# Head 0 of an attention kernel transposed on TensorE and written zero-padded, TensorE run with dummy matmuls during the first loads, and VectorE's tiles of head 0 chosen by rotation

## The chip, the cores and the metric

The kernel runs on one core of a Trainium2 chip. The metric is the device time of one execution, in microseconds (us); every figure called a time is the median of several executions. A *span* is the length of one profiled execution, about 1.7 us shorter than the time measured for the same execution. All runs of this study were in the fast state, so fast runs are compared with fast runs throughout.

Five engines matter: TensorE (PE in the profile; PEld are its weight loads), VectorE (DVE), ScalarE (ACT), GpSimd (POOL) and SyncE (SP), which here only issues DMA transfers.

## The reference

32 heads, 2048 queries and 2048 keys of 20 numbers each. Queries and keys are normalised, the scores are scaled by one number t per head, and an ordinary softmax and the product with the values follow.

```python
qn = q / (jnp.sqrt((q * q).sum(axis=-1, keepdims=True)) + eps)
kn = k / (jnp.sqrt((k * k).sum(axis=-1, keepdims=True)) + eps)
logits = jnp.einsum('bhqd,bhkd->bhqk', qn, kn) * t[None, :, None, None]
attn = _softmax(logits, axis=-1)
return jnp.einsum('bhqk,bhkd->bhqd', attn, v)
```

Because of the normalisation no score exceeds t in size, so the kernel takes exponentials without subtracting a maximum. 32 x 2048 x 2048 exponentials are the bulk of the work.

## The kernel before

Scores are made transposed: 128 keys on the partitions, 512 queries along the free axis. A head has 16 key blocks (index r) and 4 query groups (index g), so 64 pieces of 128 x 512. ScalarE takes the exponential of three pieces at a time (a *wave*, 1536 columns, out of PSUM). For 3 or 4 of the 16 key blocks VectorE does it instead, by integer arithmetic on fp16 bit patterns: one pass from PSUM (`xt`), four more in SBUF (`ee`, `ss`, `mm`, `tt`). I call the four pieces of one key block a *VectorE tile*. In the profiles `psA` holds scores for ScalarE, `psD` scores for VectorE, `p_ring` ScalarE's exponentials and `psO` the products with the values.

```python
DVE_TILES = [4 if h % 8 in (1, 4, 6) else 3 for h in range(H)]
...
    if h == 0:
        A_units += [(0, 4 * c + (g + dl) % 4, g) for dl in range(4) for c in range(na // 4) for g in range(NG)]
        rest = range(na // 4 * 4, na)
    else:
        rest = range(na)
    A_units += [(h, r, g) for r in rest for g in range(NG)]
    D_tiles += [(h, r) for r in range(na, R)]
```

A row of a transposed head has only 20 numbers, padded to 32, so four blocks are stacked on the 128 partitions. Key block r = 4c + rho lies in band rho, query group g in band g. A pair with rho = g can be multiplied directly. All other pairs need the keys *rotated* into another band (`kR`). A score matmul may use 32, 64 or 128 rows of the array; with more than 32 the queries come from `qz`, which holds group g in band g and zeros elsewhere.

```python
def qk_mm(eng, h, r, g, dst, rows):
    c, rho = divmod(r, 4)
    dl = (rho - g) % 4
    ...
    mov = qz[bt][ps, g, :] if rows > 32 else qkT[bt][ps, 0:512]
    if dl == 0:
        lhsT = qkT[bt][ps, 512 + 128 * c:512 + 128 * c + 128]
    else:
        lhsT = kR[bt][ps, dl - 1, 128 * c:128 * c + 128]
    return eng.matmul(dst, lhsT, mov, tile_position=(p0, 0))
```

Head 0 has nothing to hide behind. Before, its keys, queries and rotated keys are transposed by three DMA transposes, its first five waves are 32-row matmuls (`WPLAIN = 5`), and GpSimd clears the padding of all buffers:

```python
z_kx = memset("POOL", kx[...][:, :, D:32], 0.0, 0.8, -99)
z_qkn = [memset("POOL", qkn[i][:, :, D:32], 0.0, 0.4, -98 + i) for i in range(NN)]
z_qz = [memset("POOL", qz[i][:, :, :], 0.0, 1.8, -80 + i) for i in range(NT)]
...
trn[0] = add("SP", "trnq0", lambda e, tk: e.dma_start_transpose(
    qkT[0][:, 0:512].rearrange(...), qkn[0][:, 0:R, :].rearrange(...)), 1.3, [nq], -21, lat=2.2, dma="T0")
rot[0].append(add("SP", "trnr0", lambda e, tk: e.dma_start_transpose(
    kR[0][...], kx[:, 512:2048]), 1.3, cp, -20, lat=2.7, dma="R0"))
```

The order on each engine isn't written down. A small list scheduler simulates the engines with assumed durations and takes the ready task of lowest `pri`. It also decides which score matmuls use the full height: where the array work that it counts in a window of 3.41 us falls below `LOAD`, it raises 64-row matmuls to 128 rows. So any change of a duration or priority can also change the plan far from the place edited. That matters for two experiments below.

## Time and profile before

| | before |
|---|---|
| time, median of 3 | 748.01 us (746.55 to 749.55) |
| span of the profiled run | 745.3 us, granted clock 1.0 |
| ScalarE busy, VectorE busy, TensorE busy | 97%, 97%, 87% |
| first exponential | 14.61 us |
| ScalarE idle after that | 2.31 us, in four waits before 26.74 |
| ScalarE's last exponential ends | 741.14 us |
| VectorE's last tile ends | 737.39 us |

The last two rows are the ones to keep in mind: both engines are nearly full, and VectorE is ready 3.75 us before ScalarE. For the first stretch the clock is read off the durations of matmuls below, not off the mean granted clock.

### The profile page before, as it was taken

What the parts mean: (1) busy time and instruction counts of PE and PEld (TensorE: products, weight loads), DVE (VectorE), ACT (ScalarE), POOL (GpSimd) and SP (SyncE); (2) the same over time, 40 slices, a digit from 0 to 9 for tenths busy, and PEclk for the clock granted to TensorE, in tenths of its full rate; (3) what the DMA queues carried; (4) which work ended last, traced back from release to release, by engine and by line L of the source; (5) the groups of instructions that cost most, each with busy time, mean ns of one, the idle gap of its engine ahead of it and who ended that gap; (6) DMA issues with size and microseconds to landing.
All of it is one profiled execution on the core that took longest, in us unless ns stands there. A gap on an engine that the chain in (4) does not pass through costs nothing.

```text
span 745.3 us, 12530 instructions
## 1 busy us (share of the span) xinstructions
PE 644.9 (87%) x4960; PEld 163.4 (22%) x4960; DVE 722.0 (97%) x1321; ACT 725.7 (97%) x541; POOL 9.2 (1%) x24
## 2 busy tenths in 40 slices
PE   1988999898888989898989899899888888888886
PEld 0222222222222222222222222222222222222221
DVE  7899999999999999999999999999999999999985
ACT  2899999999999999999999999999999999999997
POOL 4000000000000000000000000000000000000000
PEclk9999999999999999999999999999999999999999
DMA  5543323233323223423233313323323323221000
GB/s 74 92 47 54 51 54 56 34 52 49 58 55 50 35 47 61 61 52 47 38 57 51 62 42 56 48 37 61 61 45 48 54 42 56 56 52 33 20 1 10
DMA packets 197930, 36.49 MB, mean 49 GB/s; under 512 B 173680, under 2 KB 197872, under 8 KB 197872
## 3 DMA queue, kind: packets, MB, share of 16 engines
q1 hardware_dynamic: 197728, 35.62, 29.9%
q8 instruction: 39, 0.64, 0.4%
q14 instruction: 19, 0.16, 0.1%
q10 hardware_dynamic: 144, 0.08, 0.0%
HBM read 7.87 MB, written 2.62 MB: 14 GB/s over the span
## 4 chain that ended last, share of the span: by engine, by line
ACT 96%; DVE 2%; PE 1%; DMA 0%; issue 0%; ACTq 0%; SPq 0%
ACT p_ring L539 96%; PE psA L462 1%; DVE sq L367 0%; DMA qk_sb<-in_k_dram 0%; DVE rs_sum L369 0%; PE psD L462 0%; PE psO L471 0%; DVE rs_u L372 0%; DVE rs_a L377 0%; ACTq L245 0%; DVE rs_b L379 0%; DVE kx L434 0%; DVE qkn L395 0%; DVE oT L483 0%; DVE xt L573 0%
## 5 line engine op out<-in xcount | busy, mean ns | idle before, releaser
L539 ACT ACTIVATE p_ring<-psA 128x1536 bf16<-128x1536 f32 x539 | 724.2, 1775 | 14.2 <-PE psA L462 14.2
L462 PE MATMUL psA<-qz,kR 64*128 64x512 bf16 (+1 forms) x1209 | 292.0, 385 | 49.4 <-ACT p_ring L539 41.2
L573 DVE TENSOR_SCALAR xt<-psD 128x512 int16<-128x512 f32 x432 | 295.0, 683 | 11.2 <-PE psD L462 8.5
L471 PE MATMUL psO<-p_ring,vaug 128*32 128x512 bf16 x1616 | 156.6, 388 | 2.4 <-ACT p_ring L539 1.3
L462 PE MATMUL psA<-qz,qkT 64*128 64x512 bf16 (+1 forms) x392 | 126.9, 383 | 15.4 <-ACT p_ring L539 12.7
L587 DVE TENSOR_TENSOR tt<-xt,mm 128x2048 f16<-128x2048 f16 x108 | 131.4, 1216 | 0.2
L462 PE MATMUL psD<-qz,kR 64*128 64x512 bf16 (+1 forms) x321 | 123.2, 384 | 4.1 <-DVE xt L573 3.1
L462 PEld LDWEIGHTS psA<-qz,kR 64*128 64x128 bf16 (+1 forms) x1209 | 63.0, 93 | 180.1 <-ACT p_ring L539 163.3
L585 DVE TENSOR_SCALAR mm<-xt 128x2048 int16<-128x2048 int16 x108 | 74.0, 685 | 0.0
L583 DVE TENSOR_SCALAR ss<-xt 128x2048 int16<-128x2048 int16 x108 | 74.0, 685 | 0.0
L581 DVE TENSOR_SCALAR ee<-xt 128x2048 int16<-128x2048 int16 x108 | 73.3, 679 | 0.3
L471 PEld LDWEIGHTS psO<-p_ring,vaug 128*32 128x32 bf16 x1616 | 39.6, 93 | 123.3 <-issue 107.7
L471 PE MATMUL psO<-tt,vaug 128*32 128x512 f16 x432 | 43.1, 389 | 4.7 <-DVE tt L587 3.7
L462 PEld LDWEIGHTS psD<-qz,kR 64*128 64x128 bf16 (+1 forms) x321 | 29.9, 93 | 73.9 <-DVE xt L573 45.4
L471 PE MATMUL psO<-ss,vaug 128*32 128x512 f16 x432 | 43.1, 389 | 0.9 <-DVE ss L583 0.3
L471 PE MATMUL psO<-ee,vaug 128*32 128x512 f16 x432 | 43.0, 388 | 0.8 <-DVE ee L581 0.4
L462 PEld LDWEIGHTS psA<-qz,qkT 64*128 64x128 bf16 (+1 forms) x392 | 31.0, 93 | 56.8 <-ACT p_ring L539 52.8
L462 PE MATMUL psD<-qz,qkT 64*128 64x512 bf16 (+1 forms) x107 | 41.3, 386 | 2.3 <-DVE xt L573 1.9
L367 DVE TENSOR_TENSOR sq<-qk_sb 128x640 f32<-128x640 bf16 x32 | 27.3, 852 | 0.5 <-DMA qk_sb<-in_q_dram 0.5
L483 DVE STREAM_TRANSPOSE oT<-psO 128x512 f32<-128x512 f32 x32 | 22.7, 710 | 4.2 <-PE psO L471 4.2
L369 DVE TENSOR_REDUCE rs_sum<-sq 128x32 f32<-128x640 f32 x32 | 25.9, 810 | 0.1
L395 DVE TENSOR_TENSOR qkn<-qk_sb,rs_r 128x640 bf16<-128x640 bf16 x31 | 25.1, 810 | 0.1
(36 smaller groups left out, 135.6 us busy)
## 6 DMA issues: line engine op xcount, KB each, us to landing
kR<-qkT SPq DMA_DIRECT2D x62, 96.0 KB, 2.1
qz<-qkT SPq DMA_DIRECT2D x128, 32.0 KB, 1.9
kR<-qkT SPq DMA_DIRECT2D x62, 64.0 KB, 2.0
qk_sb<-in_k_dram SPq DMA_DIRECT2D x32, 80.0 KB, 2.1
vaug<-in_v_dram SPq DMA_DIRECT2D x32, 80.0 KB, 3.2
qk_sb<-in_q_dram SPq DMA_DIRECT2D x124, 20.0 KB, 2.5
out_dram<-o_stage SPq DMA_DIRECT2D x31, 80.0 KB, 1.9
kR<-qkT SPq DMA_DIRECT2D x62, 32.0 KB, 1.9
```

Of the source, the lines that this page charges most:

```text
L367: s1 = dv("sq", lambda e, tk, x=x: e.tensor_tensor(sq[:, :, :], x[:, :, :], x[:, :, :], ALU.mult), 0.735, lds[h] + last_sum)
L369: sums.append(dv("sum", lambda e, tk, i=i: e.tensor_reduce(rs["sum"][:, 2 * R * i:2 * R * (i + 1)], sq[:, :, :], AXIS_X, ALU.add), 0.73, [ ...
L395: norm[h] = dv("norm", lambda e, tk, x=x, b=b, i=i: e.tensor_tensor(qkn[b][:, :, 0:D], x[:, :, :], bc(rs["r"][:, 2 * R * i:2 * R * (i + 1) ...
L462: return eng.matmul(dst, lhsT, mov, tile_position=(p0, 0))
L471: last = eng.matmul(psO[32 * g:32 * g + 32, :], vaug[h % NV][:, r_of(g), :], rhs_of(g), start=start, stop=False, skip_group_check=True, ti ...
L483: trO[h] = add("DVE", f"tr{h}", lambda e, tk: e.transpose(oT[:, :, :].rearrange("p r d -> p (r d)"), psO[:, :]), 0.63, [lambda: pv_users[h ...
L539: act[w] = add("ACT", f"exp{w}", lambda e, tk: e.activation(p_ring[:, p0 * 512:p0 * 512 + n], psA[:, slot * WAVE * 512:slot * WAVE * 512 + ...
L573: t1_prev[0] = add("DVE", f"t1.{j}.{g}", lambda e, tk, o=o: e.tensor_scalar(xt[sx][:, o:o + 512], psD[:, :], X_MUL, X_ADD, ALU.mult, ALU.a ...
L581: te = dv("e", lambda e, tk: e.tensor_scalar(ee[se][:, 0:w], x, 0x7C00, KE_BITS, ALU.bitwise_and, ALU.bitwise_or), 0.533, t1s + old("e", NE))
L583: t5 = dv("s", lambda e, tk: e.tensor_scalar(ss[se][:, 0:w], x, float(SHIFT - 4096), None, ALU.add), 0.533, t1s + old("s", NE))
L585: tm = dv("m", lambda e, tk: e.tensor_scalar(mm[sm][:, 0:w], x, 0x3FF, 0x3800, ALU.bitwise_and, ALU.bitwise_or), 0.533, t1s + old("m", NM))
L587: tT = dv("T", lambda e, tk: e.tensor_tensor(tt[se][:, 0:w], x.bitcast(FP16), mm[sm][:, 0:w].bitcast(FP16), ALU.mult), 1.067, [tm] + old(" ...
```

## The change

The intent is a faster start and a better balance. Head 0's keys and queries are transposed by TensorE against an identity matrix, and copied out by ScalarE and VectorE straight into zero-padded `qz`, so its scores are 64 or 128 rows high from the first wave. Fifteen dummy matmuls run during the loads and five more while the copies run. Head 0's VectorE tiles take key blocks "by rotation", so that the first one needs no rotated keys. The last head gets a fourth VectorE tile. Some clears move from GpSimd to VectorE. Score matmuls get absolute priority on TensorE.

```diff
-    LIGHT = 30.0
+    LIGHT = 9.0
-    PE_REST = 25.0
+    PE_REST = 6.5
+    PV_SLACK = 0.6
-    WPLAIN = 5
+    NWARM2 = 5
+    NWARM = 15
-    LEAD = 2.7
+    LEAD = 2.4
-    DVE_TILES = [4 if h % 8 in (1, 4, 6) else 3 for h in range(H)]
+    DVE_TILES = [4 if h % 8 in (1, 4, 6) or h == 31 else 3 for h in range(H)]
 (cut)
+                A_units += [(0, 12 + (g + dl) % 4, g) for dl in range(nd, 4) for g in range(NG)]
 (cut)
+                D_tiles += [(0, [12 + (g + dl) % 4 for g in range(NG)]) for dl in range(R - na)]
 (cut)
+        z_one = memset("DVE", ones[:, :], 1.0, 0.2, -99)
+        z_id = add("POOL", "id", lambda e, tk: e.affine_select(
+            ident[:, :], ones[:, 0:128], [[1, 128]], ALU.is_equal, 0.0, base=0, channel_multiplier=-1), 0.5, [z_one], -99)
+        z_kx = memset("DVE", ...)
+        z_qkn = [memset("POOL" if i else "DVE", ...) for i in range(NN)]
+        z_qz = [memset("POOL" if i else "DVE", qz[i][:, :, :], 0.0, 1.8 if i else 0.6, -80 + i) for i in range(NT)]
 (cut)
+        for i in range(NWARM):
+            warm.append(add("PE", "warm", lambda e, tk: e.matmul(psO[:, :], ones[:, 0:128], ones[:, :], ...), PE_MM, [z_one], -300))
 (cut)
+            tk_ = add("PE", "tk0", lambda e, tk: tmm(e, psD[:, :], kx[:, 0:512]), 0.35, [nk, z_id], -200)
+            tq = add("PE", "tq0", lambda e, tk: tmm(e, qdst, qsrc), 0.35, [nq, z_id], -199)
+            for i in range(NWARM2):
+                add("PE", "warm", ...)
+            trn[0] = add("ACT", "cpk0", lambda e, tk: e.activation(qkT[0][:, 512:1024], psD[:, :], ACT.Copy), 0.5, [tk_], -90)
+            for g in range(NG):   # g < 2 on ScalarE, the others on VectorE, into qz[0][gs, g, :]
 (cut)
-            rot[0] = [add("SP", "trnk0", ... dma_start_transpose ...)]
-            trn[0] = add("SP", "trnq0", ... dma_start_transpose ...)
-            qz0[:] = [dma("SP", "qz0", ...) for g in range(NG)]
 (cut)
-                       PE_MM * (1 if plain or part is pair else len(part)), deps, due_a(us[0]) - 100) for part in parts]
+                       PE_MM * (1 if part is pair else len(part)), deps, w - 10000.0) for part in parts]
 (cut)
-                        e, h, r, g, psD[:, :], tk.rows), PE_MM, dep, due - 100.05)
+                        e, h, r, g, psD[:, :], tk.rows), PE_MM, qk_deps(...) + ..., due - 20000.0)
```

## The prediction

> **What bounds the kernel now.** I read the page's busy table first, then the chain that ended last, the costliest groups, the timeline of the first 32 us, and the timeline of the last 30 us.
>
> ```profile
> PE 644.9 (87%) x4960; PEld 163.4 (22%) x4960; DVE 722.0 (97%) x1321; ACT 725.7 (97%) x541; POOL 9.2 (1%) x24
> ...
> ACT 96%; DVE 2%; PE 1%; DMA 0%; issue 0%; ACTq 0%; SPq 0%
> ...
> L539 ACT ACTIVATE p_ring<-psA 128x1536 bf16<-128x1536 f32 x539 | 724.2, 1775 | 14.2 <-PE psA L462 14.2
> ```
>
> Of 745.3 us, 96% of the chain is one instruction, ScalarE's exponential on three score tiles (1536 columns): 724.2 us over 539 of them is 1.344 us each. The idle column says that ScalarE waited 14.2 us in all, in five places. VectorE, which does 108 of the 512 score tiles by integer tricks, is just as full (97%), so there are two bounds, nearly level. The timeline shows where the 14.2 us are:
>
> ```profile
> 6.09 3.60 POOL L281 MEMSET qz<- 128x2048 bf16 x2
> ...
> 6.82 1.12 DVE L372 TENSOR_SCALAR rs_u<-rs_sum 128x32 int32<-128x32 int32 x1
> ...
> 9.54 0.49 DVE L421 TENSOR_TENSOR kx<-qk_sb,rs_r 128x320 bf16<-128x320 bf16 x1
> ...
> 11.42 1.27 SPq L439 DMA_TRANSPOSE qkT<-qkn  x1
> ...
> 12.73 1.52 SPq L442 DMA_TRANSPOSE kR<-kx  x1
> ...
> 13.95 1.03 PE L462 MATMUL psA<-qkT 32*128 32x512 bf16 x6 [13.95 <-DMA qkT<-qkn]
> ...
> 14.61 2.79 ACT L539 ACTIVATE p_ring<-psA 128x1536 bf16<-128x1536 f32 x2 [11.92 <-PE psA L462]
> ...
> 16.56 0.60 PE L462 MATMUL psD<-qkT,kR 32*128 32x512 bf16 x1 [1.58 <-DMA kR<-kx]
> ...
> 17.64 1.45 ACT L539 ACTIVATE p_ring<-psA 128x1536 bf16<-128x1536 f32 x1 [0.24 <-PE psA L462]
> ...
> 19.80 2.79 ACT L539 ACTIVATE p_ring<-psA 128x1536 bf16<-128x1536 f32 x2 [0.71 <-PE psA L462]
> ...
> 23.52 2.79 ACT L539 ACTIVATE p_ring<-psA 128x1536 bf16<-128x1536 f32 x2 [0.93 <-PE psA L462]
> ...
> 26.74 5.48 ACT L539 ACTIVATE p_ring<-psA 128x1536 bf16<-128x1536 f32 x4 [0.43 <-PE psA L462]
> ```
>
> 11.92 us pass before the first exponential, at 14.61; then come four short starvations, 0.24 + 0.71 + 0.93 + 0.43 = 2.31 us, while TensorE's matmuls last 0.60 us (0.39 from 28.26 on). After 26.74 ScalarE never idles. So everything this change can win lies in the first 27 us, in the amount of exponential work, and in the tail:
>
> ```profile
> 736.16 1.23 DVE L587 TENSOR_TENSOR tt<-xt,mm 128x2048 f16<-128x2048 f16 x1
> ...
> 741.19 0.40 PE L471 MATMUL psO<-p_ring,vaug 128*32 128x512 bf16 x4 [0.52 <-ACT p_ring L539]
> 741.64 0.72 DVE L483 STREAM_TRANSPOSE oT<-psO 128x512 f32<-128x512 f32 x1 [4.25 <-PE psO L471]
> ```
>
> VectorE finishes its last tile at 737.39 and then waits 4.25 us for ScalarE's last (ended 741.14). That is spare VectorE time which an extra VectorE tile could use.
>
> **What the Trainium skill says.** (1) "TensorE: Matmul & The Clock Gate", Part 1: TensorE starts at half clock and gets the full one after about 3.4 us of sustained work; an idle window takes it back. The trace agrees in kind: 0.60 us a matmul until about 28 us, 0.39 afterwards. The page's granted clock does not show this. (2) "VectorE: DVE Perf Modes", The three transpose paths: 128x128 takes 390 ns on TensorE, landing in PSUM, and 1309 ns by DMA. Here the DMA is dearer still: the query transpose issued at 11.42 was usable at 13.95, 2.5 us later; the rotated one took 3.8. (3) "SBUF — State Buffer", SBUF: two separate sides: VectorE in a two-port mode and GpSimd hold a shared port exclusively. The trace agrees: the tensor_scalar to rs_u took 1.12 us instead of the 0.18 of its later twins, and ended at 7.94, when GpSimd's second qz clear ended. (4) "VectorE: DVE Perf Modes", Zero memsets can be issued as uint32 (trn2): a memset costs one cycle per element. VectorE's only memset of before (32 elements, 0.09 us) can't test that.
>
> **The change part by part.**
>
> *Clears moved.* GpSimd loses kx (0.74 us), one qkn (0.42) and one qz (1.82), and gains a small select that makes the identity (I assume 0.5 us). Its 0.73 to 9.69 us shrink to about 7.6: three qkn and twelve vaug clears to about 4.0 with the identity, then two qz clears of 1.82. VectorE gains 512 + 768 + 384 + 2048 elements; at 0.96 GHz, one per cycle, that is 3.9 us (estimate from (4)), 0.9 to about 5.0, so the first square moves from 3.96 to about 5.0. That costs nothing: before, its successor started only at 5.97, because the cast in front was held by GpSimd until 5.9. The rs_u step will still be held, now to 7.6 or 7.7 instead of 7.94. Gain 0.2 us: normalised keys from 9.35.
>
> *Transposes on TensorE.* Keys normalised 9.35 to 9.84, queries to about 10.25. Four 128-column matmuls cost some 0.6 us cold (estimate: 4 x 0.107 plus the 0.17 between the cold duration 0.60 and the spacing 0.43 of the trace), so queries are in PSUM by about 10.9. Copies out: ScalarE does keys (0.6 us: 512 columns at 1.344/1536 per column plus 0.17 latency), then two query groups at about 0.5 each: 10.5 to 12.1. VectorE does the other two at 0.68 with 0.6 spacing (as the xt rows, also 512 from PSUM): done by 12.2. The first scores start at 12.2; three half-array matmuls need 0.22 + 0.39 warm, 1.03 cold; first exponential at about 12.9. Gain against 14.61: 1.7 us, the 0.2 included. Dropped: two DMA transposes and four copies of queries, all hidden except the one waited for.
>
> *Warm TensorE.* Fifteen dummy matmuls from about 1.6 us: eight at 0.43 and the rest at 0.22, to about 6.5; then 3.3 us idle until the transposes, about one window, so warmth at 12 us is likely but not sure. Five more fill the wait for the copies (1.1 us warm; 2.1 cold, which would delay the first scores by a microsecond). Warm, one wave's scores plus a VectorE score plus values fit within 1.344 us, so the 2.31 us of starvation should shrink to about 0.4: gain 1.9. The rotated keys still come by DMA: copies done about 12.8, landed about 16.6; the first wave that needs them (the fifth) is not wanted until about 17. VectorE's first tile now needs no rotation, so it no longer blocks TensorE's queue as at 16.56.
>
> *One tile moved at the end.* Head 31 goes from 3 to 4 VectorE tiles: four tile columns less for ScalarE, 1616 to 1612. That is 538 full waves and one of 1024 becoming 537 and one of 512: 1.344 + 0.427 = 1.77 us less. VectorE gains 4 x 0.605 + 3 x 0.607 + 1.2 = 5.45 us, and 1.2 for query copies.
>
> *Order on TensorE.* VectorE's scores go ahead of ScalarE's always; values are planned 0.6 us later. After 27 us ScalarE has no idle time to give back, so there is nothing to win there; VectorE's waits for scores (11.2 us in all, 5.1 of them after 690) can shrink.
>
> **Sum.** If ScalarE sets the end: 1.7 + 1.9 + 1.77 = 5.4 us. If VectorE does: from key normalisation to its last tile it took 737.39 - 9.54 = 727.9 us, some 12.9 of it idle, so 715.0 of work. After: 9.35 + 715.0 + 5.45 + 1.3 = 731.1 plus idle. ScalarE would end at 741.14 - 5.4 = 735.7. With less than about 4 us of VectorE idle ScalarE decides; I expect 6, so VectorE ends at 737.1, 1.4 us late. Net 5.4 - 1.4 = 4.0: 748.0 becomes 744.0.
>
> **Rivals.** (a) VectorE becomes the bound: with all of its 12.9 us of idle kept it ends at 744.0, the last output transpose starts 3 us later than before, and the time is 751. For it: 97% busy, and 5.1 us of its idle lies in the last heads, where no preparation fills gaps. Against: spare 4.25 us, and scores with priority. (b) The start isn't faster: GpSimd's identity is slow, or TensorE is cold again and the five dummies stand in the way; first exponential at 14, starvation kept, only the 1.77 is left: 746.5. For it: rs_u waits for GpSimd either way, and the idle gap is about one window. (c) ScalarE decides and start is fully clean: 742. (d) The new TensorE order starves ScalarE now and then in the long middle: 0.01 us in each of 538 waves is 5 us and eats the gain. Against: two PSUM slots per wave and TensorE 87% busy with pipelined matmuls.
>
> **Range and chances.** (a), (c) and a partial (b) spread a few microseconds about 744; runs of before already spread 3 us (746.55 to 749.55). Range 740.3 to 747.8. A 2% win needs 733, that is 15 us, and no part reaches it: all ScalarE idle plus 1.77 is 16. A 2% loss needs 763, which only a broken middle would give. Faster 0.01, same 0.98, slower 0.01.
>
> **What would show it.** First exponential at 12.5 to 13.4 (later than 14: rival b); ScalarE's idle after it under 1 us; matmuls of the first waves at 0.39, not 0.60; rs_u still stretched to the end of a qz clear; 537 or 538 exponentials of 1.344; VectorE's last tile ending within 3 us of ScalarE's last exponential. I am wrong if ScalarE idles after 30 us, or if VectorE's last tile ends after 740.

## The result, and the profile after

The changed kernel took **743.27 us** (median of 6 runs, 740.98 to 745.33) against 747.5 us for the kernel before in the same rounds (6 runs, 746.55 to 749.55). The ratio is 0.9941, with a 95% interval of 0.9915 to 0.9966: faster by 0.6%, and within the 2% that count as the same. Here and below a ratio is the mean time of one kernel's fast runs over that of the other's of the same rounds, so it isn't quite the ratio of the medians quoted. The profiled run took 741.79 us, with a span of 740.1 us.

The busy table, the chain that ended last and the group of exponentials, after:

```profile
PE 631.2 (85%) x4976; PEld 163.3 (22%) x4996; DVE 728.5 (98%) x1335; ACT 725.2 (98%) x543; POOL 6.6 (1%) x22
...
ACT 97%; DVE 1%; PE 1%; DMA 0%; issue 0%; ACTq 0%; DVEq 0%
...
L575 ACT ACTIVATE p_ring<-psA 128x1536 bf16<-128x1536 f32 x538 | 722.0, 1772 | 1.5 <-PE psA L496 1.5
```

ScalarE still sets the end, with one exponential fewer (538), and its idle time before exponentials fell from 14.2 us to 1.5 us. (The idle column counts from its last instruction of any kind, and ScalarE now copies just before, so this isn't the time of the first exponential.) The timeline of ScalarE alone says more in one line:

```profile
13.53 722.02 ACT L575 ACTIVATE p_ring<-psA 128x1536 bf16<-128x1536 f32 x538 [1.53 <-PE psA L496]
```

The first exponential starts at 13.53 us instead of 14.61, and from there to its end at 735.55 the timeline lists no wait of ScalarE (it merges gaps under 0.15 us). The timeline of all engines shows what happens before 13.53 (start, length, engine, instruction, count, and in brackets the idle time in front and what ended it):

```profile
1.56 5.56 PE L432 MATMUL psO<-ones 128*128 128x512 bf16 x15 [1.56 <-DVE ones L287]
...
3.69 3.57 POOL L287 MEMSET qz<- 128x2048 bf16 x2
4.09 3.21 DVE L330 CAST t_f<-tb 128x32 f32<-128x32 bf16 x1
...
4.21 3.09 DVE L381 TENSOR_REDUCE rs_sum<-sq 128x32 f32<-128x640 f32 x1
...
7.36 0.18 DVE L384 TENSOR_SCALAR rs_u<-rs_sum 128x32 int32<-128x32 int32 x1
...
9.13 0.49 DVE L439 TENSOR_TENSOR kx<-qk_sb,rs_r 128x320 bf16<-128x320 bf16 x1
...
9.68 0.61 PE L453 MATMUL psD<-ident,kx 128*128 128x128 bf16 x4 [2.57 <-DVE kx L439]
...
10.51 2.34 PE L461 MATMUL psO<-ones 128*128 128x512 bf16 x5
...
12.78 0.71 PE L496 MATMUL psA<-qz,qkT 64*128 64x512 bf16 x3
...
14.03 0.69 DVE L608 TENSOR_SCALAR xt<-psD 128x512 int16<-128x512 f32 x1
```

Four readings. First, a cast of 32 numbers takes 3.21 us: it and the sum behind it end at 7.30, when GpSimd's second clear of `qz` ends (3.69 + 3.57 = 7.26). The prediction expected this hold at `rs_u`; it sits two instructions earlier and costs the same. (In e3 below, with the same clears, the cast got in between the two: it took 1.54 us, and `rs_u` was held for 1.72 us after all, to 7.34.) Second, TensorE is cold when the transposes arrive. Four 128-column matmuls take 0.61 us, after a rest of 2.57 us since the last dummy. Third, being cold, the five dummies in front of the first scores take 2.34 us, to 12.85, while the copies that the first scores need were done about 12.0 us (ScalarE's two at 10.82 + 1.18). The scores come at 12.78. Fourth, VectorE's first tile starts at 14.03; before it was at 17.98, behind the rotated keys.

The tail, after:

```profile
734.71 1.23 DVE L622 TENSOR_TENSOR tt<-xt,mm 128x2048 f16<-128x2048 f16 x1
...
735.99 0.40 PE L511 MATMUL psO<-tt,vaug 128*32 128x512 f16 x4
736.44 0.72 DVE L523 STREAM_TRANSPOSE oT<-psO 128x512 f32<-128x512 f32 x1 [0.51 <-PE psO L511]
```

VectorE's last tile ends at 735.94 and ScalarE's last exponential at 735.55. The two engines now finish level, and VectorE, 0.39 us later, decides by a hair.

That gives a complete account of the spans, 745.3 to 740.1:

| term | before | after | gain |
|---|---|---|---|
| first exponential | 14.61 | 13.53 | 1.08 |
| ScalarE idle after it | 2.31 | 0 | 2.31 |
| exponentials themselves | 724.22 | 722.02 | 2.20 |
| ScalarE's end to the end of the span | 4.16 | 4.55 | -0.39 |
| sum | | | 5.20 |

VectorE needs an account of its own. The view that sums each engine's busy time over stretches gives it; I cut at 30, 200, 400, 600 and 700 us, from the normalisation of head 0's keys to the end of VectorE's last tile. Its sum before, then after (busy us of each engine over the whole stretch):

```profile
sum 727.85, PE 642.12 PEld 162.66 DVE 714.92 ACT 720.47 POOL 0.14; mean PE 107.02 PEld 27.11 DVE 119.15 ACT 120.08 POOL 0.02
```

```profile
sum 726.81, PE 625.22 PEld 161.27 DVE 719.51 ACT 723.67 POOL 0.00; mean PE 104.20 PEld 26.88 DVE 119.92 ACT 120.61 POOL 0.00
```

VectorE worked 4.59 us more (the extra tile, the query copies) and idled 726.81 - 719.51 = 7.30 us instead of 12.93. Its idle time paid for its new work. More than half of the difference lies at the start: before 30 us it idled 0.58 us instead of 3.54.

### The profile page after: what moved, and what is told of

Read it like the earlier page. It is cut to its first block, busy times and chain, and to the rows that moved or that the text cites. A ratio compares the mean times of both kernels' runs of the same rounds, so it can differ in the third digit from the quotient of the medians.

```text
span 740.1 us, 12574 instructions
## 1 busy us (share of the span) xinstructions
PE 631.2 (85%) x4976; PEld 163.3 (22%) x4996; DVE 728.5 (98%) x1335; ACT 725.2 (98%) x543; POOL 6.6 (1%) x22
## 3 DMA queue, kind: packets, MB, share of 16 engines
HBM read 7.87 MB, written 2.62 MB: 14 GB/s over the span
## 4 chain that ended last, share of the span: by engine, by line
ACT 97%; DVE 1%; PE 1%; DMA 0%; issue 0%; ACTq 0%; DVEq 0%
ACT p_ring L575 97%; DVE t_f L330 0%; DMA qk_sb<-in_q_dram 0%; PE psO L461 0%; DVE sq L379 0%; PE psO L511 0%; DVE oT L523 0%; PE psA L496 0%; PE psD L453 0%; DVE kx L439 0%; ACTq L249 0%; DVE o_stage L533 0%; PE psA L453 0%; DVE rs_a L389 0%; DVE rs_b L391 0%
## 5 line engine op out<-in xcount | busy, mean ns | idle before, releaser
L496 PE MATMUL psA<-qz,kR 64*128 64x512 bf16 (+1 forms) x1201 | 288.5, 384 | 70.7 <-ACT p_ring L575 65.3
L511 PE MATMUL psO<-p_ring,vaug 128*32 128x512 bf16 x1612 | 154.9, 386 | 1.4 <-issue 0.8
L496 PE MATMUL psA<-qz,qkT 64*128 64x512 bf16 x399 | 128.4, 384 | 21.9 <-ACT p_ring L575 20.9
L496 PE MATMUL psD<-qz,kR 64*128 64x512 bf16 (+1 forms) x318 | 121.6, 382 | 4.5 <-DVE xt L608 2.2
L496 PEld LDWEIGHTS psA<-qz,kR 64*128 64x128 bf16 x1210 | 63.6, 94 | 218.1 <-ACT p_ring L575 202.1
L381 DVE TENSOR_REDUCE rs_sum<-sq 128x32 f32<-128x640 f32 x32 | 28.0, 875 | 0.0
```

Source lines behind the costliest of these rows:

```text
L381: sums.append(dv("sum", lambda e, tk, i=i: e.tensor_reduce(rs["sum"][:, 2 * R * i:2 * R * (i + 1)], sq[:, :, :], AXIS_X, ALU.add), 0.73, [ ...
L511: last = eng.matmul(psO[32 * g:32 * g + 32, :], vaug[h % NV][:, r_of(g), :], rhs_of(g), start=start, stop=False, skip_group_check=True, ti ...
```

## The experiments

My theory after the result was the one of the prediction: warm TensorE ended the short starvations. The rivals were that the dummies did nothing and that the gain came from taking the rotated keys out of the way of the first VectorE tile, or from the dense zero-padded scores; and that the new priorities, which had seemed worth nothing after 27 us, held VectorE up. Other edits of the change have no experiment of their own: the planner's constants (`LIGHT`, `PE_REST`, `PV_SLACK`, `LEAD`) and the order of the first loads went along with the rest, and their share stays open. All twelve runs gave correct results. They ran in three sets, each on one chip with its own runs of the kernel before.

| run | change | median, us | ratio to before | 95% |
|---|---|---|---|---|
| e1_no_warm | after, no dummies | 742.44 | 0.9936 | 0.9923 to 0.9949 |
| e2_before_warm | before, with dummies | 747.22 | 0.9996 | 0.9983 to 1.0009 |
| e3_more_warm | after, 23 dummies first | 742.17 | 0.9931 | 0.9918 to 0.9944 |
| e4_clears_on_scalar | after, two clears on ScalarE | 742.08 | 0.9921 | 0.9905 to 0.9938 |
| e5_h31_three | after, last head 3 tiles | 742.98 | 0.9942 | 0.9922 to 0.9962 |
| e6_old_order | after, old score priorities | 749.95 | 1.0023 | 1.0015 to 1.0032 |
| e7_more_rows | after, LOAD 3328 | 756.65 | 1.0105 | 1.0086 to 1.0124 |
| e8_before_noplain | before, WPLAIN 0 | 760.67 | 1.0150 | 1.0127 to 1.0174 |
| e9_after_again | after, unchanged | 743.65 | 0.9950 | 0.9931 to 0.9968 |
| e10_clears_again | as e4 | 740.85 | 0.9913 | 0.9893 to 0.9932 |
| e11_clears_no_warm | as e4, no dummies | 739.80 | 0.9904 | 0.9886 to 0.9922 |
| e12_no_rotation | after, head 0's tiles unrotated | 752.25 | 1.0068 | 1.0054 to 1.0081 |

The kernel before had medians of 747.8 us (e1 to e4), 748.01 (e5 to e8) and 746.59 (e9 to e12).

### e1_no_warm: no dummy matmuls

```diff
-            warm.append(add("PE", "warm", lambda e, tk: e.matmul(psO[:, :], ones[:, 0:128], ones[:, :], start=True, stop=True), PE_MM,
+            warm.append(add("PE", "warm", lambda e, tk: None, PE_MM,
-                add("PE", "warm", lambda e, tk: e.matmul(psO[:, :], ones[:, 0:128], ones[:, :], start=True, stop=True), PE_MM, [tq], -198)
+                add("PE", "warm", lambda e, tk: None, PE_MM, [tq], -198)
```

The scheduler still plans the dummies but emits nothing, so all other instructions keep their order.

> The changed kernel with all 20 dummy matmuls left out, every other instruction and its order unchanged. Theory (the dummies buy a warm TensorE, at the price of standing in the queue in front of the first scores): the first scores start when the query copies are done, about 12.05 instead of 12.78 us, the first exponential at about 13.1 instead of 13.53, but the matmuls of the first waves then last 0.60 us and ScalarE starves for 1 to 3 us in the first 10 us after it; span 1 to 3 us longer than the 740.1 of the change. Rival (warmth is worth nothing, the starvation of before came from the wait for the rotated keys): no starvation, span about 0.4 us shorter.

It was not slower: 742.44 us, ratio 0.9936 against 0.9941 for the full change. ScalarE alone:

```profile
13.28 2.85 ACT L575 ACTIVATE p_ring<-psA 128x1536 bf16<-128x1536 f32 x2 [1.24 <-PE psA L496]
16.39 719.33 ACT L575 ACTIVATE p_ring<-psA 128x1536 bf16<-128x1536 f32 x536 [0.27 <-PE psA L496]
```

One starvation of 0.27 us is all that came back of 2.31. Without the five dummies in the way the first scores ran at 12.09 instead of 12.78. They were slower (1.15 us for three instead of 0.71), yet the first exponential was 0.25 us earlier. Matmuls were at 0.60 us until about 16.3 us and at 0.39 from 16.7: the zero-padded scores themselves had TensorE warm 4.5 us after they began. The theory that the dummies carry the gain falls.

### e2_before_warm: the dummies in the kernel before

```diff
+        ones = sbuf("ones", [128, 512], BF16)
+        z_one = memset("DVE", ones[:, :], 1.0, 0.2, -99)
+        for i in range(15):
+            add("PE", "warm", lambda e, tk: e.matmul(psO[:, :], ones[:, 0:128], ones[:, :], start=True, stop=True), PE_MM, [z_one], -300)
+            for i in range(7):   # in first_head, after the queries are normalised
+                add("PE", "warm", ..., PE_MM, [nq], -298)
```

> The kernel before with dummies alone added: 15 at the start, 7 after the normalised queries; all else and its order unchanged. Theory: the first exponential stays at 14.6 us (it waits for the DMA transpose), the four later starvations of 2.31 us in all shrink to 0.3 to 1.0 us, since the matmuls last 0.39 instead of 0.60 us; span about 743.7 instead of 745.3. Rival (the wait for the rotated keys and the queue order cause them): at least 1.5 us of starvation left, span within 0.8 us of 745.3.

Ratio 0.9996, nothing. The timeline of all engines shows why:

```profile
13.96 0.60 PE L471 MATMUL psA<-qkT 32*128 32x512 bf16 x6 [0.46 <-DMA qkT<-qkn]
...
16.57 0.60 PE L471 MATMUL psD<-qkT,kR 32*128 32x512 bf16 x1 [2.00 <-DMA kR<-kx]
...
17.63 1.45 ACT L548 ACTIVATE p_ring<-psA 128x1536 bf16<-128x1536 f32 x1 [0.45 <-PE psA L471]
```

TensorE was warm at 13.96: six matmuls in 0.60 us, where before they took 1.03. Then the queue reached VectorE's first score, which needs the rotated keys, and everything behind it stood for 2.00 us. At 16.57 one matmul took 0.60 us again. Seven starvations followed, 4.04 us in all (0.45, 0.72, 0.92, 0.43, 0.26, 0.52, 0.74), more than the 2.31 of the kernel before. In this run warmth didn't last across that wait and the 32-row waves behind it. The profiled execution was the slowest of the five (748.99 us), so how many of the later starvations the others had isn't known.

### e3_more_warm: 23 dummies instead of 15

```diff
-    NWARM = 15
+    NWARM = 23
```

> The changed kernel with 23 instead of 15 first dummies, nothing else changed. Theory (TensorE went cold again in the 2.6 us between 7.1 and 9.68, so the five later dummies ran at 0.43 us each and held up the first scores): the dummies end near 8.9, TensorE is still warm at 9.68, the five later dummies take 1.1 instead of 2.3 us, the first scores start at 12.05 when the copies are done, first exponential at about 12.7 instead of 13.53, span about 0.8 us shorter. Rival (the copies set the start, not the dummies): first exponential stays at 13.5.

The dummies now run until 8.97 and TensorE is warm at the transposes: four in 0.40 us, the five dummies in 1.24, the first exponential at 12.40. That is the start that the prediction had drawn. ScalarE alone:

```profile
12.40 4.28 ACT L575 ACTIVATE p_ring<-psA 128x1536 bf16<-128x1536 f32 x3 [0.80 <-PE psA L496]
16.91 1.45 ACT L575 ACTIVATE p_ring<-psA 128x1536 bf16<-128x1536 f32 x1 [0.23 <-PE psA L496]
18.85 716.68 ACT L575 ACTIVATE p_ring<-psA 128x1536 bf16<-128x1536 f32 x534 [0.49 <-PE psA L496]
```

But 1.13 us at the start didn't reach the end: the span was 740.1, as without it. By 16.4 us matmuls were at 0.6 us again, ScalarE waited 0.23 and 0.49 us, and its end came at 735.53 against 735.55. The median (742.17) can't be told from e1's or from the change's.

### e4_clears_on_scalar and e10_clears_again: the last two clears off GpSimd

```diff
-        z_qz = [memset("POOL" if i else "DVE", qz[i][:, :, :], 0.0, 1.8 if i else 0.6, -80 + i) for i in range(NT)]
+        z_qz = [memset("DVE", qz[i][:, :, :], 0.0, 0.6, -80) if i == 0 else add("ACT", "zq", lambda e, tk, i=i: e.activation(
+            qz[i][:, :, :], <ones, 4 x 512>, ACT.Copy, scale=0.0), 1.8, [z_one], -94 + i) for i in range(NT)]
```

ScalarE, idle then, writes the zeros as ones times zero.

> The changed kernel with the two qz clears of GpSimd done by ScalarE in its idle time (a copy of ones times zero), nothing else changed. Theory ([...]the cast of t, and with it the row sums behind it, are held to 7.30 us by GpSimd's two clears of 1.8 us): the cast takes under 0.3 us, the sums end at about 5.05, keys normalised from about 6.9 instead of 9.13, TensorE's idle gap vanishes so that the later dummies run warm, first exponential at about 10.4 instead of 13.53, span about 737. Rival (the cast waits for the load of t, or something else): sums still end near 7.3 and the first exponential stays at 13.5.

The same four VectorE steps in e4's timeline:

```profile
3.97 0.18 DVE L330 CAST t_f<-tb 128x32 f32<-128x32 bf16 x1
4.09 0.82 DVE L381 TENSOR_REDUCE rs_sum<-sq 128x32 f32<-128x640 f32 x1
...
4.94 0.18 DVE L384 TENSOR_SCALAR rs_u<-rs_sum 128x32 int32<-128x32 int32 x1
...
6.73 0.49 DVE L439 TENSOR_TENSOR kx<-qk_sb,rs_r 128x320 bf16<-128x320 bf16 x1
```

The cast takes 0.18 us and not 3.21, and the keys are normalised at 6.73 instead of 9.13. TensorE has then rested 0.32 us only and is warm, so the first exponential starts at 10.19, 3.34 us earlier. This shows that GpSimd's clears held VectorE, and what they cost: 2.40 us at the keys, the rest through a TensorE that is now warm at the transposes and the dummies. The profiled span was 738.0. The median was 742.08: four of its six executions had a granted clock of 0.991 to 0.993 and took 742.08 to 743.17 us; the other two (0.996) took 739.6 and 739.7.

> The qz clears on ScalarE again (as in e4), now beside the changed kernel. Theory (the earlier start carries through): first exponential at 10.2, 3.3 us ahead of 13.53, median 1 to 3 us below that of the changed kernel on this chip; not the whole 3.3, since in e4 a half-clock window at 377 us cost 0.73 us. Rival (the gain at the start is taken back later by more such windows): medians within 0.7 us.

A repeat in another set gave 740.85 against 743.65 for the change itself (e9), 2.8 us less. First exponential at 10.28, span 737.8. The two intervals, 0.9893 to 0.9932 and 0.9931 to 0.9968, just touch.

### e5_h31_three: the last head with three VectorE tiles

```diff
-    DVE_TILES = [4 if h % 8 in (1, 4, 6) or h == 31 else 3 for h in range(H)]
+    DVE_TILES = [4 if h % 8 in (1, 4, 6) else 3 for h in range(H)]
```

> The changed kernel with head 31 back at three VectorE tiles. Theory (ScalarE's work bounds, VectorE's spare time at the end takes the fourth tile): ScalarE has 539 exponentials again, ends 1.8 us later relative to its first exponential (723.8 instead of 722.0 us after it), VectorE then waits about 6 us for the last values as it did before (4.25 there), span about 741.5 against 740.1 at equal clock. Rival (the fourth tile only moves the end from ScalarE to VectorE): span within 0.5 us of 740.1.

The medians don't resolve it: 742.98, ratio 0.9942. In the trace ScalarE's unbroken stretch has 539 exponentials and lasts 724.12 us instead of 722.02; VectorE then waits 8.23 us for the last product before it transposes the output. So the tile takes about 2 us off ScalarE and uses VectorE's spare time, but at the end 740.8 stands against 740.1, with a start that happened to be 0.93 us earlier in this run (12.60).

### e6_old_order: scores with the priorities of before

```diff
-  ... deps, w - 10000.0) for part in parts]
+  ... deps, due_a(us[0]) - 100) for part in parts]
-  ... qk_users[0][:2 if j == 0 else 0], due - 20000.0)
+  ... qk_users[0][:2 if j == 0 else 0], due - 100.05)
```

> The changed kernel with the old order of scores on TensorE (by due time, VectorE's not always first); plans of the later order follow from it, so other instructions move too. Theory (VectorE's scores first is what lets the fourth tile of head 31 fit): VectorE's idle time for scores rises from 6.6 to 9 us or more, its last tile ends 2 to 4 us after ScalarE's last exponential instead of 0.4, span 742 to 744 at a clock of 0.998 or more. Rival (the order matters nowhere): span 740 to 741. Another reading, that the old order has more 128-row matmuls (252 planned against 116) and so keeps the clock up: mean clock at least 0.998 in every run, where the change had 0.989 to 1.0.

749.95 us, ratio 1.0023: the whole gain is gone, and a little more. ScalarE is hardly to blame. It starts at 13.10, waits 0.66 us once, and ends at 736.38. The last output transpose, and VectorE's sum over the same kind of stretch (9.13 to 743.89):

```profile
744.61 0.72 DVE L523 STREAM_TRANSPOSE oT<-psO 128x512 f32<-128x512 f32 x1 [0.72 <-PE psO L511]
```

```profile
sum 734.76, PE 654.55 PEld 169.30 DVE 723.27 ACT 724.16 POOL 0.00; mean PE 109.09 PEld 28.22 DVE 120.54 ACT 120.69 POOL 0.00
```

VectorE's last tile ends at 743.89, 7.5 us after ScalarE. It idled 11.49 us, 4.19 more than in the change, and was busy 3.76 us more with the same instructions, of nearly the same mean durations. Most of that second part is lost overlap: two VectorE instructions in a row lie 0.60 us apart though each lasts 0.68, and the busy time counts the overlap once. An instruction that has to wait for its score loses that overlap as well. (Added up one by one, the durations over the stretch grew by 1.16 us, 818.44 to 819.60, so 2.60 of the 3.76 us are overlap.) So here the idle column shows little more than half of what VectorE lost.

One caution: the plan followed the priorities, and it put 252 score matmuls at full height, against 96 in the change (116 in the expectations, with the twenty dummies) and 124 before. How much of the 7 us is the order and how much those rows, this run can't tell. The expectation's last reading, that these rows keep the clock up, fails: all 15 executions had 0.989 to 0.996.

### e7_more_rows: more full-height matmuls

```diff
-    LOAD = 3072.0
+    LOAD = 3328.0
```

The executions of the change differ by 4 us with their granted clock, so I asked whether more rows would hold the clock up.

> The changed kernel with the planner's demand on TensorE's load raised by a twelfth, which turns 490 instead of 116 score matmuls into full-height ones (zero-padded rows, same results). Theory (the change's runs spread over 4 us because TensorE falls to half clock for single windows of about 3.4 us in mid-run, seen as clocks of 0.989 to 1.0, each window costing ScalarE some 0.7 us): clock 0.998 or more in every run, times within 2 us of each other, median at most 742. Rival (full-height matmuls can't run beside each other and cost TensorE's time): ScalarE or VectorE waits more for scores even at full clock, span over 741.

The opposite: 756.65 us, clock 0.983 to 0.991, some 490 full-height score matmuls. In the trace TensorE stood for 1.63 us at 48 us waiting for VectorE, was at half clock from 51 to 61, and ScalarE starved five times by 0.49 to 1.18 us. The theory is refuted. VectorE in turn was waiting for a load: it sat idle for 1.63 us, to 48.42, until a head's queries had landed. So this plan differs by more than its rows, and what full height costs by itself isn't shown.

### e8_before_noplain: the kernel before with zero-padded scores from the start

```diff
-    WPLAIN = 5
+    WPLAIN = 0
```

> The kernel before without its five first waves of 32-row matmuls: they use the zero-padded queries and 64 rows from the first wave on, and so wait for the copies of the queries by DMA. Theory (32-row matmuls and the wait for rotated keys keep TensorE at half clock until 28 us, while 64- and 128-row ones warm it within some 4 us as in the changed kernel without dummies): first exponential at about 17.6 us, 3 us later than 14.61, but the starvation after it shrinks from 2.31 to under 1 us and matmuls are at 0.39 us by about 22; span about 746.5 to 747.5. Rival (the clock has other causes): matmuls at 0.60 until 27 us or later, starvation still over 2 us.

760.67 us, and not for the reason tested. The first exponential came at 19.51 instead of the 17.6 that I had expected, and the plan that followed had two stretches at half clock in mid-run (42 to 53 and 588 to 597 us) with starvations of up to 2.62 us. Both followed late loads: VectorE waited 2.33 us, to 41.03, and 1.15 us, to 584.54, for a head's queries. The first time TensorE then stood behind VectorE:

```profile
42.51 0.60 PE L462 MATMUL psD<-qz,kR 64*128 64x512 bf16 x1 [2.60 <-DVE xt L573]
```

So the part of the zero-padded scores without the rest of the change was not isolated. But the start of this trace bears on the theory of warmth. ScalarE made its first 16 exponentials, from 19.51 to 41.39, without a wait that the timeline lists, although matmuls lasted 0.60 us until about 27: with zero-padded scores and the rotated keys there before the first of them, half clock alone didn't starve ScalarE here. In e3 it did (0.23 and 0.49 us).

### e9_after_again: the change, once more

> The changed kernel as it is, run again beside the next three so that they share a chip and its runs of before. Expected from its first six runs (740.98 to 745.33) and from the three variants whose start alone differs: median 742 to 743.5, ratio 0.992 to 0.995. ScalarE's stretch from first exponential to last end 722 us where the clock is 0.998 or more, longer where it is lower.

743.65 us, ratio 0.9950, in line with the first measurement. Two things in its trace explain the spread. At the start TensorE was warm at the transposes by chance (0.40 us for four), although it had rested 3.19 us, longer than the 2.57 after which it was cold in the first run; its first exponential came at 12.61. And in mid-run two windows of half clock cost ScalarE 0.81 and 0.36 us. The busy view by stretches, with the granted clock as the third number from the right, and ScalarE's line after it:

```profile
489.20:492.60 3.40, 2.61 (x17) 0.61 (x16) 3.40 (x8) 3.40 (x4) 0.00 (x0) 1.00 0.48 46
493.00:495.50 2.50, 2.50 (x20) 0.43 (x16) 2.10 (x4) 2.36 (x2) 0.00 (x0) 0.50 0.49 29
```

```profile
496.16 180.11 ACT L575 ACTIVATE p_ring<-psA 128x1536 bf16<-128x1536 f32 x134 [0.81 <-PE psA L496]
```

The slower of the fast runs had, roughly, the lower clocks: six executions of the change had spans of 739.2 (clock 1.0), 740.1 (0.998), 740.5 (0.995), 742.9 (0.992), 743.6 (0.991) and 742.5 (0.989). What starts such a window stays open. Just before this one TensorE was busy 2.61 us of 3.40, a little less than elsewhere, but not idle.

### e11_clears_no_warm: clears on ScalarE and no dummies

The edits of e4 and e1 together.

> As e10, with all 20 dummy matmuls left out as well. Theory (e1: the dummies are worth nothing, since dense scores warm TensorE by themselves within some 5 us): first exponential at 10.6 to 10.8 (cold scores), 0.2 to 0.6 us of starvation until about 15, span within 1 us of e10's 738.0. Rival (with the idle gap gone the dummies do help): span 739.5 or more, starvation over 1 us.

**739.80 us**, ratio 0.9904 (0.9886 to 0.9922): the fastest version, 3.85 us below the change on the same chip (743.65), with intervals that don't overlap. Its first exponential is at 10.87, and its five runs lie within 1.9 us. ScalarE's first lines:

```profile
10.87 2.85 ACT L575 ACTIVATE p_ring<-psA 128x1536 bf16<-128x1536 f32 x2 [1.24 <-PE psA L496]
13.99 252.98 ACT L575 ACTIVATE p_ring<-psA 128x1536 bf16<-128x1536 f32 x188 [0.27 <-PE psA L496]
```

Against e10, with the dummies, it can't be told apart. So it beats both kernels, and the dummies may be left out.

### e12_no_rotation: head 0's VectorE tiles as before

```diff
-                A_units += [(0, 12 + (g + dl) % 4, g) for dl in range(nd, 4) for g in range(NG)]
+                A_units += [(0, r, g) for r in range(12, na) for g in range(NG)]
-                D_tiles += [(0, [12 + (g + dl) % 4 for g in range(NG)]) for dl in range(R - na)]
+                D_tiles += [(0, [r] * NG) for r in range(na, R)]
```

> The changed kernel with head 0's VectorE tiles as before (rows 13 to 15 for all groups, which need the rotated keys that come by DMA near 15 us), ScalarE's units to match; the planner then puts all 12 unrotated ScalarE units ahead of VectorE's first score. Theory (rotation lets VectorE start its tiles 2 to 3 us sooner, and VectorE is level with ScalarE at the end): VectorE's first tile piece starts near 17 instead of 14.03, it fills the time with preparing heads 1 and 2, the end moves by under 1 us. Rival (VectorE's lost start is carried to the end): last output transpose 2 us or more after ScalarE's last exponential, span over 742 at a clock of 0.998.

752.25 us, ratio 1.0068: 8.6 us worse than the change on the same chip. VectorE's first piece starts at 18.19 instead of 14.03, and ScalarE waits 0.50 and 0.23 us. VectorE's first piece, and its sum from 9.15 to the end of its last tile at 746.85:

```profile
18.19 0.69 DVE L608 TENSOR_SCALAR xt<-psD 128x512 int16<-128x512 f32 x1 [0.93 <-PE psD L496]
```

```profile
sum 737.70, PE 658.61 PEld 170.79 DVE 724.26 ACT 724.18 POOL 0.00; mean PE 109.77 PEld 28.46 DVE 120.71 ACT 120.70 POOL 0.00
```

VectorE idles 13.44 us instead of 7.30 and is busy 4.75 us more with the same instructions. It ends 9.8 us behind ScalarE (737.02) and sets the end. Between 9.15 and 30 us it did 17.93 us of work, in the change 20.29; so 2.4 us of the loss arise at the start, where the rotation acts, and the rest later, where the plan changed with it (312 full-height matmuls). Only the first part is shown to be the rotation's.

## Why the prediction was right or wrong

**The total was right.** 744.0 was predicted and 743.27 measured, inside the range, and the class (same) too. It rested on two ends: ScalarE's at 735.7 (735.55 in the profile) and VectorE's at 737.1 (735.94). That picture, two level engines of which VectorE decides late, is what the profile shows. The single terms were less good than their sum. That the median agrees within a microsecond is partly luck: the profiled execution gained 5.2 us and not 4.0, and slower executions, with half-clock windows in mid-run that the sum doesn't contain, took back about as much.

**Start, 1.7 predicted, 1.08 measured.** Keys were normalised at 9.13 (9.35 predicted). The step that failed was "Five more fill the wait for the copies (1.1 us warm; 2.1 cold, which would delay the first scores by a microsecond)", where I had called warmth likely. In the profiled run TensorE was cold and they took 2.34 us; e1 shows that they delayed the scores by 0.69 us. In e9 it happened to be warm, and the first exponential came at 12.61, within the 12.5 to 13.4 predicted; 13.53 of the profiled run lies just outside. The signpost "later than 14: rival b" wasn't reached.

**Starvation, 1.9 predicted, 2.31 measured, for another reason.** "Warm, one wave's scores plus a VectorE score plus values fit within 1.344 us" gave the credit to the dummies. e1 shows that they are not needed: without them 0.27 us come back. e2 shows that they don't suffice: with them, the kernel before still loses 4.04 us. What stands in their place is the remark that I made in passing, that VectorE's first tile no longer blocks TensorE's queue, together with scores that are zero-padded from the first wave and warm TensorE by themselves. Of these two, the wait is shown in e2's trace (0.45 us of starvation right behind it) and in e12, where 0.73 us came back with it. The rest falls to the zero-padded scores by elimination only: their own share wasn't isolated. Nor is it shown that they work by warmth, since e8 starved nothing in its first waves at half clock.

**Less exponential work, 1.77 predicted, 2.20 measured.** How much of it is the tile's stays open. If the tile gave its 1.77, the other 0.43 would fit the number of stretches: an exponential that starts a stretch lasts 1.45 us against 1.344 in a row, and before had five stretches, after one, so 4 x 0.106 = 0.42. This is only argued, and e5 speaks against it: with 539 exponentials in one stretch it lasted 724.12 us, where this would give 723.8. By e5 the tile itself is worth 2.10.

**VectorE's overrun, 1.4 predicted, 0.39 measured.** Idle was 7.30 rather than 6 us. The work was 719.5 rather than 715.0 + 5.45 + 1.3 = 721.75, 2.2 us less. I had taken the 715.0 us of busy time as fixed, though part of it was probably overlap lost to waits; e6 and e12 show busy time growing by 3.76 and 4.75 us with the same instructions. The clears on VectorE cost about 2.0 us (0.48 + 0.38 + 0.22 + 0.91) and not 3.9. Those of zeros run as uint32 with half the elements, which the Trainium skill states in the section that point (4) of the prediction names, and which I had overlooked; the trace shows them so (`128x1024 uint32` for `qz`). They were off the critical path.

**Still held by GpSimd, right in time and wrong in place.** VectorE was held to 7.30, as predicted within 0.4 us; but the cast of t was held, not `rs_u`. What I hadn't asked is what it was worth: e4 shows 3.34 us at the first exponential, more than the change gained there; without dummies it is 2.41 us (13.28 in e1, 10.87 in e11).

**"After 27 us ScalarE has no idle time to give back, so there is nothing to win there"** was the weakest sentence. It fits what the timeline lists of ScalarE and overlooks VectorE. e6 and e12 show that rival (a), VectorE as the bound at about 751, was one edit away: undoing either the priorities or the rotation gives 749.95 and 752.25. The idle that I expected to shrink did shrink (12.93 to 7.30), more than half of it before 30 us, and this is what lets ScalarE's gains reach the end. Rivals (b) and (d) did not come: the start was faster, and ScalarE didn't idle after 30 us in the profiled run. A mild form of (d), 0.4 to 0.8 us now and then at half clock, occurs in other executions. They may be what lies between (c), 742, and the median.

## What to carry to other kernels

When two engines are level, ask of every change what it does to the one that doesn't set the end. A few us of waits there undo the gain, and the idle column needn't show all of their cost: in e6 4.19 us of 7.95. Test warm-up work by leaving it out with the order unchanged; here twenty dummy matmuls were worth nothing, and the real work warmed the engine. Clears on GpSimd beside VectorE's first steps held VectorE 2.40 us here, so give them to an engine that is idle then.

## What the Trainium skill lacked or had wrong

- "TensorE: Matmul & The Clock Gate": it explains a lost clock by idle gaps, short ones between groups of matmuls included, and calls the transitions run-variable. The runs agree with the latter (cold after a rest of 2.57 us in one run, warm after 3.19 us in another), though 2.57 us is shorter than the idle window of about 3.4 us that it gives. It names no share of busy time below which a working TensorE loses its clock, and the share alone doesn't settle it here: in e9 the clock was 0.50 from 493.0 to 495.5 us, after 3.4 us in which TensorE had been busy 2.61 us; in the change it was 1.00 from 16.4 to 19.7 us, after 3.4 us with 2.20 us busy.
- "SBUF — State Buffer": it describes the lock between VectorE and GpSimd for single instructions. It doesn't say that the loser may wait through several: a cast of 32 elements took 3.21 us, to the end of the second of two consecutive GpSimd clears (together 3.57 us), and a reduce issued behind it, 0.82 us by itself, took 3.09 us. In e3 the cast came through after the first (1.54 us).
- "VectorE: DVE Perf Modes", Zero memsets can be issued as uint32: it gives one cycle per element. VectorE's clears of 192, 384 and 1024 elements took 0.22, 0.38 and 0.91 us, which is 0.83 ns for each further element, where one cycle at the prediction's 0.96 GHz would be 1.04 ns.
- On no page that I read: what a wait on VectorE costs beyond its idle time, because it also loses the overlap of consecutive instructions (0.68 us long, 0.60 apart). In e6, 4.19 us more idle came with 3.76 us more busy time for the same instructions, 2.60 of it lost overlap.
